# Attention and a squared-ReLU layer on one core: each store of two half blocks of tokens as two transfers of 64 rows

## The chip, the core and the metric

The kernel runs on one NeuronCore of a Trainium2 chip. The core has a matrix engine (TensorE, PE in the profile, its weight loads PEld), a vector engine (VectorE, DVE), a scalar engine (ScalarE, ACT), a general one (GpSimd, POOL), and a queue processor (SyncE, SP) that only issues transfers. Transfers run on 16 DMA engines that all queues share. The metric is device microseconds of one launch; lower is better.

## What is computed

Sliding-window attention with linear distance biases (8 sequences, 8 heads, 576 positions, head size 64, window 128), then a two-layer network on all 4608 tokens, with ReLU squared between the layers. Everything comes and goes in float32.

```python
scores = scale * np.matmul(q, k.transpose(0, 1, 3, 2))
mask = (rel >= 0) & (rel < window)
scores = np.where(mask, scores + bias[None], -1000000000.0)
attn = softmax(scores)                      # written out in the original
x = np.matmul(attn, v) ...reshape(B * S, H * D)      # 4608 x 512
h = x @ w_in                                # 512 x 2048
r = np.maximum(h, 0.0)
return (r * r) @ w_out                      # 2048 x 512
```

## The kernel before, in words

**Blocks and ranges.** Each sequence of 576 tokens is four blocks of 128 tokens and a half block of 64. The kernel pairs the half blocks of two sequences, so that they fill one range of 128 columns together: `ranges` holds 36 ranges of 128 tokens, 32 of them one block each and four of them two half blocks (ranges 14, 21, 28 and 32). Four ranges make a group of 512 tokens, and there are nine groups, 0 to 8. The half blocks thus stand in group 3 (third range), 5 (second), 7 (first) and 8 (first).

**Stages.** For each block PE multiplies q and k (line 643), ACT takes the exponential (L670), DVE multiplies by the mask of biases (L678), PE multiplies by v (L750), and DVE divides by the sums (L778) into a tile `x`. GpSimd loads k, q and v and casts them to bfloat16 on the way (L523, L528). From block 8 on, SP transposes k and q by DMA into `kqT` (L569, `DMA_TRANSPOSE`) and `x` into `xT` (L785). The first layer, "up", is lines 897, 915 and 996; from group 6 on it uses Strassen's seven products in Winograd's form, for which DVE makes differences of `xT` in tiles `ut` (L963). ACT and DVE make ReLU and square. The second layer, "down", is L1072 for group 0 and, from group 1 on, Strassen's seven products again (`product`, L1176), with sums of the activations made by DVE (L1297).

**Down and its stores.** Each product of a group adds into one of the output's quarters, 256 tokens by 256 columns. DVE or ACT copies or adds these into a tile `osb` of 128 partitions by 512 float32: its first 256 columns belong to one range of 128 tokens, its second 256 to the next. Each finished quarter is stored by `store` inside `product` (L1205 to L1214): products 2 and 3 finish the two column halves of a group's first two ranges, products 7 and 4 those of its last two. `places` says where the rows go. When both ranges are plain blocks at a fitting distance, one transfer covers (row, range, column), 256 KB. Otherwise each range has a transfer of its own, 128 KB in rows of 1 KB: a plain block is 128 rows of `out`, and a range of two half blocks is one transfer over (half, row, column), L1114 to L1116: the two halves stand d rows apart in `out`, and together they are the 128 partitions of the tile's half. There are eight such transfers, two for each of the four half-block ranges; in their pattern on the side of `out` the half, of size 2, is the outermost dimension.

Seven of the eight are issued by SP; the one of group 8's product 3 is issued by ACT (`end`). The last group's last product goes to `last_product`, which stores its two ranges, both plain blocks, in three pieces (L1274), two from SP and one from ACT. Stores of group 0 are at L1098.

**What sets the order.** The whole program is first a list of tasks, each with the engines that could run it, a cost in ns, a key, the tasks that it needs and the buffers that it takes and frees. `Plan.order` (L167 to L263) goes through them as a list scheduler: on each engine it takes, of the tasks that could start, the one with the smallest key. A table `ADJ` moves single keys. The result is a fixed order of instructions for each engine. For a transfer, the cost in `engs` is how long its queue is taken to be busy (530 for a store, 1200 to 1500 for a transpose), and `dma` is how long the transfer is taken to fill the DMA engines:

```python
            if t.dma is not None:
                at = max(st + self.FIRST[e], self.dma_free)
                self.dma_free = at + t.dma
                t.end = self.dma_free + (self.LAND[e] if t.lat is None else t.lat)
            ...
            free[e] = st + dur
```

A tile `osb` (a ring of five) is free again at the store's planned `end`; on the chip, when the store has landed. Each queue issues in its order: when an issue waits or takes long, what is behind it waits too. Transfers from SP and ACT take turns with eight semaphores, so each also waits until the transfer eight before it has landed.

Of the kernel before, what the change touches and what calls it, by code (L numbers as in the profile page):

```python
# [266 lines left out]
def kernel(  # L267
    ctx: ExitStack, tc: tile.TileContext, q, k, v, moe_w_in, moe_w_out, out
):
    nc = tc.nc  # L270
# [29 lines left out]
    at = {x: m for m, x in enumerate(seq)}  # L300
# [43 lines left out]
    plan = Plan({**psum_bufs, "rec": 4, "rt": RT, "g": 2, "osb": OSB, "cs": CS, "ut": 2, "s1": 1, "s2": 1, "v0": B, "kqT0": B, "stage": 2, **size})  # L344

    def bank(slot, name):
        slot.tile = psum.tile([128, 512], FP32, tag=slot.tag, bufs=psum_bufs[slot.tag], name=name)
        return slot.tile
# [18 lines left out]
    def dve_p(n, rate=1):  # L367
        return n / rate / 0.96 + 72.0

    def mm(n):  # L370
        return max(n, 66) / 2.4 + 2.5
# [36 lines left out]
    for part in (1, 0):  # L408
        key = EARLY + 2 if part else -1e5 + 1100
# [127 lines left out]
    for what, key in at_first.items():  # L537
        n = int(what[1:])
# [563 lines left out]
    def places(r, n):  # L1102

        rows = [[b * S + kb * 128 for b, kb in ranges[r + i]] for i in range(n)]
        if n == 2 and len(rows[0]) == len(rows[1]) == 1:
            lo, d = rows[0][0], rows[1][0] - rows[0][0]
            if d >= 128 and lo + 2 * d <= NT:
                return [((0, 1), lambda w: out[lo:lo + 2 * d, w].rearrange("(j p) c -> p j c", p=d)[0:128])]
        to = []
        for j, x in enumerate(rows):  # L1110
            if len(x) == 1:
                to.append(((j,), lambda w, x=x: out[x[0]:x[0] + 128, w]))
            else:
                d = x[1] - x[0]  # L1114
                lo = x[0] + 64 - d
                to.append(((j,), lambda w, lo=lo, d=d: out[lo:lo + 2 * d, w].rearrange("(h p) c -> h p c", p=d)[:, d - 64:d]))  # L1116
        return to

    t_ws = []
# [24 lines left out]
    def product(g, p, z, key):  # L1144
# [60 lines left out]
        def store(name, t, hi, tok, end=False):  # L1205
            so = st["slot"][name]
            w = slice(hi * 256, hi * 256 + 256)
            for i, (j, to) in enumerate(places(4 * g + tok, 2)):
                def run(j=j, to=to):
                    (nc.scalar if end else nc.sync).dma_start(  # L1210
                        to(w), so.tile.rearrange("p (j c) -> p j c", j=2)[:, j[0]] if len(j) == 1 else
                        so.tile.rearrange("p (j c) -> p j c", j=2))
                plan.add({"ACTQ" if end else "SP": 530.0}, key, run, [t], [], [so], dma=340.0 * len(j), lat=1000.0,
                         name=f"st{g}.{p}.{tok + i}")  # L1214

        def combine(name, what, deps, free, tok, hi, label, end=False):
            so = st["slot"][name]

            def run():
                what(so.tile)  # L1220
            t = plan.add({"DVE": dve_p(512)}, key, run, deps, [], free, name=f"{label}_{g}")
            store(name, t, hi, tok, end)
            return t

        if p == 1:
            snap("s1", [])
        elif p == 2:
            combine("s1", lambda o: nc.vector.tensor_tensor(o, slot.tile, o, op=ALU.add), both + [st["s1"]], [slot],
                    0, 0, "c11")
        elif p == 6:  # L1230
            snap("s2", [])
        elif p == 5:
            snap("s5", [])
        elif p == 7:
            if g == NG - 1:
                snap("s3", [slot])
            st["c22"] = combine("s5", lambda o: nc.vector.tensor_tensor(o, slot.tile, o, op=ALU.add),
                                both + [st["s5"]], [slot], 2, 1, "c22")
        elif p == 3:
            combine("s2", lambda o: nc.vector.tensor_tensor(o, slot.tile, o, op=ALU.add), both + [st["s2"]], [slot],  # L1240
                    0, 1, "c12", g == NG - 1)
        else:
            snap("s3", [slot])
            store("s3", st["s3"], 0, 2)

    def last_product(g, z, key, st, stationary):

        F = FCB // 2
        cuts = [(0, 256)] if z == 0 else [(0, LAST), (LAST, 256)]
        for lo, hi in cuts:  # L1250
            slot = Slot("a")

            def emit(slot=slot, lo=lo, hi=hi):
                bank(slot, "o")
                for c in range(F):
                    nc.tensor.matmul(slot.tile[:, 0:hi - lo], stationary(c), wsum[:, 3, c, lo:hi],
                                     start=c == 0, stop=c == F - 1)
            tm = plan.add({"PE": F * mm(hi - lo)}, key, emit,
                          g_sq_at(g)(1, (2, 3)) + [t_ws[0][3], t_ws[1][3], st["P", 3, 1], st.get("tail")],
                          [slot], [g_slots[g]], name=f"p{g}.4.{z}" + ("b" if lo else ""))  # L1260
            st["tail"] = tm
            so = st["slot"]["s3"]

            def run(slot=slot, lo=lo, hi=hi):
                o = so.tile[:, z * 256 + lo:z * 256 + hi]
                nc.vector.tensor_tensor(o, o, slot.tile[:, 0:hi - lo], op=ALU.add)
            t = plan.add({"DVE": dve_p(hi - lo)}, key, run, [tm, st["s3"]], [], [slot],
                         name=f"c21.{z}.{lo}_{g}")

            q = z == 1 and lo == 0  # L1270

            def store(lo=lo, hi=hi, q=q):
                to = places(4 * g + 2 + z, 1)[0][1]
                (nc.scalar if q else nc.sync).dma_start(to(slice(lo, hi)), so.tile[:, z * 256 + lo:z * 256 + hi])  # L1274
            plan.add({"ACTQ" if q else "SP": 530.0}, key, store, [t], [], [so], dma=340.0 * (hi - lo) / 256, lat=1000.0,
                     name=f"st{g}.4.{z}" + ("b" if lo else ""))

    def g_sq_at(g):
        def sq(half, parts):
            return [x for t in (2 * half, 2 * half + 1) for p in parts for x in sq_of[g, t, p]]  # L1280
        return sq
# [76 lines left out]
```

## Time and profile before

| | |
|---|---|
| three runs | 305.5, 305.91, 306.91 us (median 305.91) |
| the profiled execution, whole | 305.41 us |
| its span, first to last instruction | 303.5 us |
| PE busy | 288.1 us (95%) |
| DVE, ACT, POOL busy | 241.6, 205.7, 106.4 us |
| mean granted clock of PE | 0.997 |
| stores of lines 1205 to 1214 | 37 from SP, 2 from ACT |
| issue time of those from SP: least, median, most | 0.345, 0.532, 3.582 us |
| landing of those that the profile tells: least, median, most | 1.7, 2.1, 12.9 us |
| last PE instruction, last DVE instruction end | 296.9, 297.2 us |

Times within the execution are in us from the span's start. The profile has a page and further views of the same trace: who waited for whom, the chain of work that ended last, the instructions in order of time, and tables by stretches of time. In them a row names line, engine, operation, and the tiles written and read (out<-in); "SPq" and "ACTq" are queue instructions, which only issue a transfer. The difference between span and whole time, 1.9 us, lies around the program.

### The profile page before, as it was taken

The numbers are of one execution on the slowest core, as the hardware profiler recorded it, in microseconds if no ns is written. First come the engines' busy times: TensorE is split into PE (matmuls) and PEld (weight loads), VectorE is DVE, ScalarE is ACT, GpSimd is POOL, SyncE is SP. The second block draws the span as 40 slices with busy tenths as digits, with TensorE's granted clock in tenths as the row PEclk, the third lists the DMA queues.
The fourth block names the chain that finished last, engine by engine and source line by source line (L and its number), as shares of the span: only waits on it lengthen the run. The fifth ranks groups of instructions, "written<-read, shape, count | busy, mean of one in ns | idle before, by whom it ended". The sixth has DMA issues, their size and how long they took to land.

```text
span 303.5 us, 8328 instructions
## 1 busy us (share of the span) xinstructions
PE 288.1 (95%) x3311; PEld 224.8 (74%) x3311; DVE 241.6 (80%) x624; ACT 205.7 (68%) x394; POOL 106.4 (35%) x132
## 2 busy tenths in 40 slices
PE   6989999997999999999999999899999999999991
PEld 2679755986887887556657866468898888888880
DVE  4584666779985899798969993999999998899841
ACT  3685444577486674894988567696997689789510
POOL 8953398263462774525725502360000000000000
PEclk9999999999999999999999999999999999999998
DMA  9999999999999999999999999999203301110223
GB/s 132 145 202 206 184 187 165 150 156 154 160 160 183 160 162 157 189 153 133 164 155 164 178 145 74 192 151 184 86 14 103 48 35 41 67 35 2 85 71 90
DMA packets 170312, 39.62 MB, mean 131 GB/s; under 512 B 156320, under 2 KB 169760, under 8 KB 170272
## 3 DMA queue, kind: packets, MB, share of 16 engines
q0 software_dynamic: 115184, 18.10, 84.6%
q1 hardware_dynamic: 54382, 20.39, 44.2%
q10 hardware_dynamic: 706, 0.59, 0.7%
q8 instruction: 26, 0.43, 0.6%
q14 instruction: 14, 0.11, 0.2%
HBM read 36.70 MB, written 9.44 MB: 152 GB/s over the span
## 4 chain that ended last, share of the span: by engine, by line
PE 73%; DMA 16%; POOL 4%; DVE 3%; SPq 1%; issue 1%; ACT 0%; POOLq 0%; DVEq 0%
PE o L1176 31%; PE h L996 12%; PE h L915 12%; DMA w_out_sb<-in_moe_w_out_dram 6%; PE h L897 6%; DMA xT<-x 5%; PE pv L750 5%; PE s L643 5%; DMA vf<-in_v_dram 3%; DMA w_in_sb<-in_moe_w_in_dram 2%; POOL kq L523 2%; POOL vf L528 2%; DVE x L778 1%; PE o L1072 1%; SPq L785 1%
## 5 line engine op out<-in xcount | busy, mean ns | idle before, releaser
L858 ACT ACTIVATE rt<-h 128x512 bf16<-128x512 f32 (+1 forms) x109 | 64.3, 597 | 37.3 <-PE h L897 17.5
L670 ACT ACTIVATE P<-s 128x512 bf16<-128x512 f32 x120 | 64.2, 605 | 9.6 <-PE s L643 9.6
L1176 PEld LDWEIGHTS <-g 128*128 128x128 bf16 x624 | 59.8, 98 | 9.3
L523 POOL DMA_DIRECT2D kq<-in_k_dram x39 | 33.3, 854 | 73.4 <-DMA kqT<-kq 65.6
L870 DVE TENSOR_TENSOR g<-rt 128x512 bf16<-128x512 bf16 (+1 forms) x99 | 40.8, 418 | 18.8 <-ACT rt L858 16.8
L1176 PE MATMUL o<-w_out_sb,g 128*128 128x256 bf16 x384 | 47.5, 273 | 0.0
L897 PE MATMUL h<-xT,w_in_sb 128*128 128x128 bf16 (+1 forms) x512 | 46.6, 246 | 0.5 <-DMA xT<-x 0.5
L915 PE MATMUL h<-xT,w_in_sb 128*128 128x512 bf16 x192 | 46.0, 380 | 0.0
L897 PEld LDWEIGHTS <-w_in_sb 128*128 128x128 bf16 x512 | 38.6, 98 | 4.7 <-issue 0.7
L678 DVE TENSOR_TENSOR P<-P,masks 128x512 bf16<-128x512 bf16 x96 | 39.0, 421 | 3.1 <-ACT P L670 0.9
L523 POOL DMA_DIRECT2D kq<-in_q_dram x39 | 33.2, 851 | 7.5 <-PE h L897 3.8
L1176 PE MATMUL o<-wsum,sums 128*128 128x256 bf16 x256 | 31.6, 273 | 1.2 <-DVE sums L1297 1.2
L778 DVE TENSOR_TENSOR x<-pv,rec 128x256 bf16<-128x256 f32 (+1 forms) x80 | 31.3, 415 | 0.6
L528 POOL DMA_DIRECT2D vt<-in_v_dram x32 | 26.9, 850 | 13.6 <-PE pv L750 11.0
L1176 PE MATMUL o<-wsum,g 128*128 128x256 bf16 x240 | 30.7, 273 | 0.0
L915 PEld LDWEIGHTS <-w_in_sb 128*128 128x128 bf16 x192 | 17.3, 98 | 17.6
L868 ACT ACTIVATE g<-rt 128x512 bf16<-128x512 bf16 x46 | 29.0, 632 | 1.3
L1176 PEld LDWEIGHTS <-sums 128*128 128x128 bf16 x256 | 24.5, 98 | 4.8 <-DVE sums L1297 1.4
L750 PEld LDWEIGHTS <-P 128*128 128x128 bf16 (+1 forms) x576 | 22.8, 100 | 6.0 <-issue 2.1
L1017 DVE TENSOR_TENSOR vf<-h,vf 128x512 f32<-128x512 f32 x36 | 24.4, 688 | 2.9 <-PE h L996 1.1
L858 ACT ACTIVATE rt<-vf 128x512 bf16<-128x512 f32 x36 | 22.3, 625 | 3.6 <-DVE vf L1017 3.6
L377 ACT ACTIVATE osb<-o 128x512 f32<-128x512 f32 x19 | 11.4, 598 | 17.2 <-PE o L1176 17.2
(82 smaller groups left out, 392.6 us busy)
## 6 DMA issues: line engine op xcount, KB each, us to landing
out_dram<-osb SPq DMA_DIRECT2D x27, 256.0 KB, 3.1
kq<-in_k_dram POOLq DMA_DIRECT2D x31, 128.0 KB, 7.7
kq<-in_q_dram POOLq DMA_DIRECT2D x31, 128.0 KB, 8.8
vt<-in_v_dram POOLq DMA_DIRECT2D x24, 128.0 KB, 8.6
w_out_sb<-in_moe_w_out_dram POOLq DMA_DIRECT2D x4, 512.0 KB, 16.2
out_dram<-osb SPq DMA_DIRECT2D x15, 128.0 KB, 7.3
w_in_sb<-in_moe_w_in_dram POOLq DMA_DIRECT2D x3, 512.0 KB, 12.4
vf<-in_v_dram POOLq DMA_DIRECT2D x8, 128.0 KB, 6.0
```

The costliest lines, as they stand in the source:

```text
L523: nc.gpsimd.dma_start(view(kq[s_kq[m].idx], i), source(src, m, split))
L528: nc.gpsimd.dma_start(tile_of(s_v[m])[0:n, :, 0:D], source(v, m))
L670: nc.scalar.activation(flat(Pt[sP.idx]), sS[i].tile.rearrange("p (j t) -> p j t", j=2)[:, :, lo:hi], AF.Exp, bias=0.0, scale=scale)
L678: nc.vector.tensor_tensor(flat(Pt[sP.idx]), flat(Pt[sP.idx]), flat(masks), op=ALU.mult)
L750: nc.tensor.matmul(sv.tile[0:n, hi * (D + 1):(hi + 1) * (D + 1)], prob, tile_of(s_v[mk])[:, h, 0:D + 1], start=mk == parts[0][1], stop=mk ...
L778: nc.vector.tensor_tensor(o, heads(sv)[0:n, :, 0:D], sr.tile[0:n, :].unsqueeze(2).to_broadcast([n, 4, D]), op=ALU.mult)
L858: nc.scalar.activation(srt.tile[:, 0:n], i, AF.Relu, bias=0.0, scale=1.0)
L870: nc.vector.tensor_tensor(o, i, i, op=ALU.mult)
L897: nc.tensor.matmul(slot.tile[:, f * w:(f + 1) * w], w_in_sb[:, cc, fc * 128:(fc + 1) * 128], xT[:, cc, lo % (XR * 128):lo % (XR * 128) + w ...
L915: nc.tensor.matmul(slot.tile, w_in_sb[:, cc, fc * 128:(fc + 1) * 128], xT[:, cc, g * 512 % (XR * 128):g * 512 % (XR * 128) + 512], start=c ...
L996: nc.tensor.matmul(slot.tile[:, j * 256:j * 256 + 256], a, b_, start=fresh and j == 0 and c == 0, stop=c == 1, skip_group_check=True)
L1176: nc.tensor.matmul(slot.tile[:, z * 256:z * 256 + 256], stationary(c), moving(c), start=fresh and z == 0 and c == 0, stop=c == F - 1, skip ...
```

## The change

A range of two half blocks is stored as two transfers of 64 rows each, one for each half, in place of one transfer over (half, row, column). `places` now gives for each transfer of `store` a list of (first partition, partitions, rows of `out`): one entry for a plain block or a pair of blocks, two entries for two half blocks. `store` issues them one behind the other from the same queue, and the planner's cost of such a store on its queue becomes 530 for each entry (its `dma` cost stays). In `last_product` the loop has one entry, as both its ranges are plain.

```diff
             if d >= 128 and lo + 2 * d <= NT:
-                return [((0, 1), lambda w: out[lo:lo + 2 * d, w].rearrange("(j p) c -> p j c", p=d)[0:128])]
+                return [((0, 1), [(0, 128, lambda w: out[lo:lo + 2 * d, w].rearrange("(j p) c -> p j c", p=d)[0:128])])]
         to = []
         for j, x in enumerate(rows):
-            if len(x) == 1:
-                to.append(((j,), lambda w, x=x: out[x[0]:x[0] + 128, w]))
-            else:
-                d = x[1] - x[0]
-                lo = x[0] + 64 - d
-                to.append(((j,), lambda w, lo=lo, d=d: out[lo:lo + 2 * d, w].rearrange("(h p) c -> h p c", p=d)[:, d - 64:d]))
+            n = 128 // len(x)
+            to.append(((j,), [(n * i, n, lambda w, r=r, n=n: out[r:r + n, w]) for i, r in enumerate(x)]))
         return to
...
                 def run(j=j, to=to):
-                    (nc.scalar if end else nc.sync).dma_start(
-                        to(w), so.tile.rearrange("p (j c) -> p j c", j=2)[:, j[0]] if len(j) == 1 else
-                        so.tile.rearrange("p (j c) -> p j c", j=2))
-                plan.add({"ACTQ" if end else "SP": 530.0}, key, run, [t], [], [so], dma=340.0 * len(j), lat=1000.0,
+                    parts = so.tile.rearrange("p (j c) -> p j c", j=2)
+                    for p, n, at in to:
+                        (nc.scalar if end else nc.sync).dma_start(
+                            at(w), parts[p:p + n, j[0]] if len(j) == 1 else parts[p:p + n])
+                plan.add({"ACTQ" if end else "SP": 530.0 * len(to)}, key, run, [t], [], [so], dma=340.0 * len(j), lat=1000.0,
                          name=f"st{g}.{p}.{tok + i}")
...
             def store(lo=lo, hi=hi, q=q):
-                to = places(4 * g + 2 + z, 1)[0][1]
-                (nc.scalar if q else nc.sync).dma_start(to(slice(lo, hi)), so.tile[:, z * 256 + lo:z * 256 + hi])
+                for p, n, at in places(4 * g + 2 + z, 1)[0][1]:
+                    (nc.scalar if q else nc.sync).dma_start(at(slice(lo, hi)),
+                                                            so.tile[p:p + n, z * 256 + lo:z * 256 + hi])
```

## The prediction

> **What bounds the kernel now.** I began with the page's slices, to see which engine has no rest and where:
>
> ```profile
> PE   6989999997999999999999999899999999999991
> ...
> DMA  9999999999999999999999999999203301110223
> ```
>
> TensorE (PE) stands at 9 nearly everywhere, so from the fifth slice on only a hole in PE can be won. The end is different: in the last slice PE is at 1, while DMA still works. Next I asked who waited. The answers, for PE and for VectorE (DVE) from 100 us on and for SyncE's queue (SP) over the whole run, hold these rows:
>
> ```profile
> PE s L643 <- DVE x L778: 1.5, 1, 1.5
> ...
> DVE ut L963 <- DMA xT<-x: 4.9, 1, 4.9
> ...
> SPq L1353 <- DMA out_dram<-osb: 4.5, 1, 4.5
> ```
>
> PE has one hole after 100 us, of 1.5 us; DVE stood still for 4.9 us for a transpose of x; and at the end SP waits 4.5 us for stores. The chain of waits between 180.86 and 193.6 us ties the first two together:
>
> ```profile
> 180.86 8.78 DMA xT<-x
> ...
> 189.76 0.44 DVE ut L963
> ...
> 191.94 0.98 DVE x L778 x3
> 192.93 0.61 PE s L643 x16
> ```
>
> One transpose issued at 180.86 takes 8.78 us. DVE is stuck behind it, works off its queue, and PE gets its operands at 192.93 (the hole is 1.47 us, 191.44 to 192.91).
>
> **What the stores have to do with it.** The table by stretches says how many DMA engines work; its last two columns are the busy share of 16 engines and GB/s:
>
> ```profile
> 255.45:256.45 1.00, 1.00 (x12) 0.90 (x10) 0.69 (x2) 1.00 (x3) 0.00 (x0) 1.00 0.74 262
> 179.00:184.20 5.20, 5.20 (x55) 2.97 (x54) 4.62 (x14) 4.89 (x10) 0.74 (x1) 1.00 1.39 41
> 217.00:220.50 3.50, 3.50 (x61) 2.96 (x59) 3.37 (x9) 3.40 (x8) 0.00 (x0) 1.00 0.12 37
> ...
> 300.25:302.00 1.75, 0.00 (x0) 0.00 (x0) 0.00 (x0) 0.00 (x0) 0.00 (x0) 0.93 0.12 39
> ```
>
> At 255.45 a whole store of two blocks (256 KB, outermost dimension 128) moves in 1 us. At 217 us a store over (half, row, column) is alone on the queue (issued 216.04, 128 KB): 0.12 x 16 = 1.9 engines, 3.5 us, 37 GB/s. Two engines do 64 rows each, as many as its outermost dimension, the half. The other two rows run at the same rate: 179 to 184.2 us (issued 171.59; the share there is swollen by long records of other packets, the 41 GB/s are what counts), and the end of the program. A single block of 128 rows, issued 229.88, landed after 1.7 us. So eight stores, two halves times four half blocks, sit on two of sixteen engines.
>
> The Trainium skill, "DMA: Bandwidth & Descriptors", section "Why a DMA increments its semaphore by 16 and not by 1", says that the engines used are the largest number up to 16 that divides the slowest dimension of both sides; for (2, 64, c) that is 2, which the 1.9 engines agree with, and for 64 rows it would be 16.
>
> **The change part by part.** *Issues.* Eight issues become sixteen. In quiet stretches one over the halves takes 0.53 to 0.55 us on SP, a plain block alone 0.345, behind another 0.45 to 0.47. Two plain ones are 0.80 at the middle of these, so +0.25 us of SP each. On SP this lies beside PE work: SP is off PE's path except through its transposes. If the cover went, seven times 0.25 would be 1.8 us.
>
> *The stage at 168 us* (group 3: two half stores, two plain ones, one pair).
>
> ```profile
> 168.54 7.26 SPq L1210 DMA_DIRECT2D out_dram<-osb  x5
> 175.91 6.88 SPq L785 DMA_TRANSPOSE xT<-x  x3
> 182.96 5.72 SPq L569 DMA_TRANSPOSE kqT<-kq  x2
> ```
>
> Five stores take 7.26 us here because the plain block behind each half store takes 1.61 and 3.58 us to issue. The transposes follow at once, and between 179.0 and 184.2 us nothing but the two-engine store moves (41 GB/s, in a queue that before and after does 170 to 280). The new stores have the rows outermost, as the plain block that landed in 1.7 us has; from that row I take it that 64 rows spread too, 4 to an engine. So the queue should come free about 5 us earlier (184.2 less 179.0), and the transpose that landed at 189.64 also. PE could run at 191.44; it needs 1.5 us of these 5. I take the whole hole, **-1.47**. Bounds: 0, if the queue stays clogged by the loads (DMA is at 9 in these slices), and -1.47, since PE is busy for 102.88 of the 102.9 us from 194 us to its end and nothing more can be won. Late next would be PE's own product behind it, for which the operands are there. The half stores of groups 5 and 7 have no waiter: the transposes at 233 to 237 us are used at 260, and PE has no hole.
>
> *The end.* The last issues are these:
>
> ```profile
> 294.75 0.37 SPq L1210 DMA_DIRECT2D out_dram<-osb  x1
> ...
> 295.87 1.54 ACTq L1210 DMA_DIRECT2D out_dram<-osb  x2
> 296.02 0.74 DVE L1266 TENSOR_TENSOR osb<-osb,o 128x256 f32<-128x256 f32 x2 [0.18 <-PE o L1256]
> 296.51 1.07 SPq L1274 DMA_DIRECT2D out_dram<-osb  x2
> 296.92 0.29 DVE L1266 TENSOR_TENSOR osb<-osb,o 128x128 f32<-128x128 f32 x1 [0.16 <-PE o L1256]
> 297.51 0.41 ACTq L1274 DMA_DIRECT2D out_dram<-osb  x1
> ```
>
> The half store is ScalarE's (ACT) first at 295.87 (1.14 us to issue, then 0.36 for the plain one). By the landing events fourteen engines finish the very last store at 300.2 to 300.7, the other two at 301.8 and 302.2: on those it queues behind 64 rows. The issue at 297.23 needs 4.8 us to land where alone 1.7 (one block) to 2.1 (a pair) is usual. After the change ACT issues three. The first takes between 0.36 (a plain one) and 1.14 (today's); I take 0.95, since 0.19 of today's 1.14 is what the form costs more on SP (0.54 against 0.345) and the rest looks like ACT's first issue since the program's start. With 0.36 for each of the next two and today's gaps, the last issue goes out at 297.7 (between 297.1 and 297.9). With 1.9 us to land (1.7 to 2.7, the last being what today's fourteen engines need) it is done at 299.6 in place of 302.2: **-2.5** (bounds -1.6 to -3.1; in the warm case SP's issue at 297.23 is the last). What follows, 1.3 us to 303.5, stays.
>
> *The order.* The planner is told 530 ns more for each split SP store. Following its rules through its own list, I find that the entry behind is the pair's other part, or starts later than the longer issue ends, but for group 5's last store (+0.4 us); no transpose moves. Only the places of the last ACT and SP issues change. I cost this at 0; what hides it is that SP has gaps there. A moved order would cost up to the holes PE had when it waited for masks and sums at 73 to 76 us (0.8 + 1.2).
>
> *Sum.* 1.47 + 2.5 = 4.0. The profiled execution took 305.41 (span 303.5), so 301.4. The three runs have a median of 305.91, 0.5 higher; I add half of that and forecast **301.7 us**.
>
> **Rivals.**
> *The end alone:* the hole at 192 stays, because the loads keep the DMA engines full. For it: DMA at 9 until 205 us. Against: 41 GB/s where that store is alone. 305.4 - 2.5 + 0.25 = 303.2.
> *The hole alone:* three issues on ACT and a late landing eat the end (last issue 297.9, landing 2.7 and a second of contention). 304.2.
> *It does not spread:* 64 rows could be put on few engines; no run here has a plain store of 64 rows. Then only issues are added, +0.36 on ACT: 306.1, the same.
> *Halves serialize:* the Trainium skill, same page, section "Rules for kernel authors", advises against two transfers to disjoint halves, since both spread over the same sixteen engines, and for one of 128 rows. As a mechanism of this kernel it would add an issue and gain no landing, 305.4 + 0.36 + 0.25 = 306.0, if today's store used sixteen engines; the 1.9 engines speak against it.
> *Slower:* the long issues at 169 and 172 us belong to the full queue and not to the half store ahead, so that each added issue takes as long. Two more of 3.58 us put the transpose of 189.64 at 196.8, and PE's hole grows by 7.2: 305.4 + 7.2 - 2.5 = 310.1. It decides from a delay of 2.5 us on. Against: another plain store of a pair in a full queue, at 207.29, took 1.38, and issues behind no half store at 112 to 115 us, also in full slices, 0.54 to 0.61.
>
> **How the numbers follow.** Forecast 0.65, the end alone 0.16, the hole alone 0.07, no spread or serialized halves 0.07, slower 0.05. The range takes the forecast's bounds (305.4 - 1.47 - 3.1 = 300.8) and the first rival with its own (305.9 - 1.6 = 304.3, of which I leave the last third out): 300.7 to 304.0. What can be told from no change here is 0.5%, 1.5 us, so faster means below 304.4: forecast, the end alone, most of the hole alone, 0.87; same 0.08; slower 0.05.
>
> **What would show it.** Right: no stretch left in which only about two engines move (179 to 184, 217 to 220.5, 300 to 302 above); no DVE wait of 4.9 us at L963 and no PE hole at L643; SP's last wait for stores near 2 us and not 4.5. Wrong: the issues of the seven stores at 168 us together longer than 7.26 us; landings of the last stores still over 4 us; or new PE holes between 100 and 290 us, which would mean that the order changed.

## The result, and the profile after

The kernel after takes 301.65 us (median of four runs, 301.38 to 302.25), the kernel before 306.3 us beside it (305.5 to 306.91): a ratio of 0.9853, 95% interval 0.9822 to 0.9883, so 4.5 us less (3.6 to 5.5). The two profiled executions are 305.41 and 301.38 us, their spans 303.5 and 299.5. No computation changed, and the order of instructions on every engine is that of before, apart from the added issues; the lines after `places` have moved up by a few (L1176 is now L1172, L1210 is L1208, L1274 is L1271).

The slices of the page after, to be held against those of before:

```profile
PE   6989999997999999999999999999999999999994
```

The reader is to see two digits in PE's row: the 8 in the 26th slice, where the hole was, is a 9, and the last slice has a 4 in place of a 1, since the span ends sooner after PE's end. Asked who waited from 100 us on, the profile has no row for PE any more, and none for DVE at L963. What is left of SP's wait for the last stores is

```profile
SPq L1351 <- DMA out_dram<-osb: 1.8, 1, 1.8
```

which was 4.5. The stretches show what became of the two-engine transfers (stretch and length; per engine busy time and count; granted clock, busy share of the 16 DMA engines, GB/s):

```profile
179.00:184.20 5.20, 5.20 (x55) 2.95 (x54) 4.62 (x15) 4.89 (x11) 0.50 (x1) 1.00 1.72 142
...
296.00:298.00 2.00, 0.00 (x0) 0.00 (x0) 0.00 (x0) 0.00 (x0) 0.00 (x0) 1.00 0.76 242
```

142 GB/s stand where there were 41, and in the last two microseconds of the stores 242 GB/s at a share of 0.76, where the end of before had 39 at 0.12. The issues of the stage at 168 us in order of time:

```profile
169.05 4.20 SPq L1208 DMA_DIRECT2D out_dram<-osb  x7
174.64 4.65 SPq L785 DMA_TRANSPOSE xT<-x  x3
```

Seven stores take 4.20 us where five took 7.26, and the transposes behind them are issued in 1.2 to 1.4 us each; the last of the three for `xT` lands at 183.68, against 189.64. Of these 6.0 us, 2.8 are its earlier issue (178.07 against 180.86) and 3.2 its shorter way from issue to landing (5.61 against 8.78). DVE is not held up, and PE runs through. The end:

```profile
294.58 1.86 ACTq L1208 DMA_DIRECT2D out_dram<-osb  x3
...
296.55 0.38 ACTq L1271 DMA_DIRECT2D out_dram<-osb  x1
```

ACT now issues three transfers in 1.86 us, so its last issue goes out 0.97 us after PE's end (295.58) and not 0.63 us after it; it lands in 1.6 us.

The 4.03 us between the two profiled executions divide at PE's end: it comes 1.30 us earlier (296.88 to 295.58: the same matmuls start 0.24 us later than before from 102 us on, ahead of every changed store, and 1.30 us earlier from 195.5 us on, so 1.54 us go with the hole), and from PE's end to SP's last wake-up it is 2.63 us and not 5.36, so 2.73 us less.

### The profile page after: what moved, and what is told of

Its sections match the earlier page's. It is cut to its first block, busy times and chain, and to the rows that moved or that the text cites. A ratio compares the mean times of both kernels' runs of the same rounds, so it can differ in the third digit from the quotient of the medians.

```text
span 299.5 us, 8343 instructions
## 1 busy us (share of the span) xinstructions
PE 288.5 (96%) x3311; PEld 224.6 (75%) x3311; DVE 241.9 (81%) x624; ACT 205.8 (69%) x394; POOL 106.5 (36%) x132
## 4 chain that ended last, share of the span: by engine, by line
PE 80%; DMA 11%; POOL 4%; DVE 2%; issue 1%; ACT 1%; POOLq 0%
PE o L1172 32%; PE h L915 14%; PE h L996 12%; PE h L897 9%; DMA w_out_sb<-in_moe_w_out_dram 6%; PE pv L750 6%; PE s L643 5%; DMA vf<-in_v_dram 3%; DMA w_in_sb<-in_moe_w_in_dram 2%; POOL kq L523 2%; POOL vf L528 2%; PE o L1072 1%; PE o L1253 1%; DVE x L778 0%; DVE g L870 0%
## 5 line engine op out<-in xcount | busy, mean ns | idle before, releaser
L1172 PEld LDWEIGHTS <-g 128*128 128x128 bf16 x624 | 59.8, 98 | 9.3
L1172 PE MATMUL o<-w_out_sb,g 128*128 128x256 bf16 x384 | 47.5, 273 | 0.0
L1172 PE MATMUL o<-wsum,sums 128*128 128x256 bf16 x256 | 31.6, 273 | 1.2 <-DVE sums L1295 1.2
L1172 PE MATMUL o<-wsum,g 128*128 128x256 bf16 x240 | 30.7, 273 | 0.0
L1172 PEld LDWEIGHTS <-sums 128*128 128x128 bf16 x256 | 24.5, 98 | 4.8 <-DVE sums L1295 1.4
```

The source lines that it names most:

```text
L1172: nc.tensor.matmul(slot.tile[:, z * 256:z * 256 + 256], stationary(c), moving(c), start=fresh and z == 0 and c == 0, stop=c == F - 1, skip ...
```

## The experiments

Times of before scatter by about a per cent from run to run, so each ratio stands with its interval, and the trace is read for what it shows exactly: the hole and the wait at the end. Part of the scatter lies ahead of every changed store: in the fourteen traces PE is idle for about 4.5 to 7.2 us in the first 100 us. Each ratio is against runs of before taken beside the experiment; their medians are 305.28 us (for the end, group 3, the other five and the cut by columns), 305.75 (62 rows, quarters, ACT's queue, SP's share) and 305.84 (the control and the three runs with it). The quotient of the medians differs from the ratio by up to 0.3%. "Last wait" is SP's for the stores; "tail" is the time from PE's end to its last wake-up.

**Which of the eight stores matter.** Three kernels split some of them only:

```diff
-    def places(r, n):
+    def places(r, n, split=False):
...
-            n = 128 // len(x)
-            to.append(((j,), [(n * i, n, lambda w, r=r, n=n: out[r:r + n, w]) for i, r in enumerate(x)]))
+            if len(x) == 1 or split:
+                n = 128 // len(x)
+                to.append(((j,), [(n * i, n, lambda w, r=r, n=n: out[r:r + n, w]) for i, r in enumerate(x)]))
+            else:
+                d = x[1] - x[0]
+                lo = x[0] + 64 - d
+                to.append(((j,), [(0, 128, lambda w, lo=lo, d=d: out[lo:lo + 2 * d, w].rearrange("(h p) c -> h p c", p=d)[:, d - 64:d])]))
...
-            for i, (j, to) in enumerate(places(4 * g + tok, 2)):
+            for i, (j, to) in enumerate(places(4 * g + tok, 2, (g, p) == (8, 3))):
```

This is the end alone; for the stage at 168 us the condition is `g == 3`, for the other five stores `g in (5, 7) or (g, p) == (8, 2)`. The diffs of the experiments are against the kernel after, but for one, which says so.

*The end alone.* Expected:

> Only group 8's product 3, the store that ACT issues at the end, is split in two halves of 64 rows; the other seven keep the form of before. Theory (two places, independent): SP's last wait falls from 4.5 to about 1.9 us, the hole of 1.5 us at PE's scores stays, 306.3 - 2.7 = 303.6 us. Rival (the gain at the end is one gain with the middle, for instance a matter of all eight): 301.7 or 306.3 us.

Measured: 303.76 us, ratio 0.9919 (0.988 to 0.9959), 2.5 us less by the ratio and 1.5 by the medians. PE waited (from 100 us on: line, what ended the wait, us in total, times, longest)

```profile
PE s L643 <- DMA kqT<-kq: 2.1, 1, 2.1
```

and SP for the stores

```profile
SPq L1356 <- DMA out_dram<-osb: 1.9, 2, 1.7
```

The hole is there, the last wait is short. The end is a gain of its own.

*The stage at 168 us alone.* Expected:

> Only the two stores of group 3's half-block range (the stage at 168 us) are split; the other six keep the form of before. Theory: the wait of DVE for the transpose of x (4.9 us at L963) and the hole of 1.5 us in PE go, the last wait of SP stays at 4.5 to 4.6 us; 306.3 - 1.4 = 304.9 us. Rival (the hole comes from the loads that fill the DMA engines, and went for another reason): hole stays, 306.3 us.

Measured: 304.37 us, ratio 0.9974 (0.9942 to 1.0006). In the trace DVE has no wait at L963 and PE no hole after 100 us, and the last wait is that of before:

```profile
SPq L1356 <- DMA out_dram<-osb: 4.4, 2, 4.2
```

The mechanism came out, the size of it not clearly: 0.8 us, and the interval holds both nothing and 1.4. It was run again (below).

*The other five.* Expected:

> Only the stores of groups 5 and 7 and the one of group 8's product 2 are split, five of the eight. Theory: nobody waits for them, so 306.3 us, within 0.3; hole and last wait as before. Rival (five stores that land earlier free tiles and the queue for something): 0.5 us or more below that.

Measured: 304.76 us, ratio 0.9965 (0.9936 to 0.9993), 1.1 us less by the ratio and 0.5 by the medians, where nothing was expected. The trace gave no reason in the changed stores: hole of 0.96 us, DVE's wait of 4.1 us at L963, last wait 4.3. So this too was run again.

**The same once more, with a control.** The kernel before against itself:

> The kernel before, unchanged, against itself: ratio 1.000. How far the ratio and the interval stray from that says how much a difference of 0.3% to 0.4% in the other runs is worth.

The kernel after:

> The kernel after, unchanged, on this chip: ratio 0.9853 as before (0.982 to 0.988), 4.0 to 4.5 us less than the kernel before; no hole of PE after 100 us, last wait 2.6 us after PE's end.

The other five, and group 3:

> The same kernel as the one in which only the five stores of groups 5, 7 and 8 (product 2) are split, which came out at 0.9965 (0.9936 to 0.9993) where 1.000 was expected. Theory (nobody waits for these five): ratio 1.000, within 0.003, and in the trace hole and last wait as before. Rival (they bring something, for instance because the last store's queue is empty earlier): 0.9965 again, and a last wait that is shorter than that of the kernel before in the same call by 0.5 us or more.

> The same kernel as the one in which only the two stores of group 3 are split, which came out at 0.9974 (0.9942 to 1.0006) where 0.9953 (1.4 us) was expected. Theory (the hole of 1.47 us goes, all of it is won): 0.995, 1.4 us. Rival (the hole goes, but half of it comes back as other idle time of PE): 0.9975, and in the trace more idle time of PE elsewhere.

Measured, in this order: 0.9994 (0.9958 to 1.003), 0.9873 (0.9829 to 0.9917), 0.9988 (0.9955 to 1.0021), 0.9944 (0.9915 to 0.9973). In the traces, the kernel after again has no hole, and a tail of 2.59 us; that of the other five has a hole of 1.02 us and a tail of 5.37 us, against 5.49 in the control; that of group 3 has no hole. So the other five bring nothing that can be told from the control (0.24% as a mean of two runs, so a small gain is not excluded), and group 3 alone is worth 0.41% as a mean of its two runs, 1.25 us. The parts add up: 0.81% at the end and 0.41% at 168 us are 1.2%, against 1.5 and 1.3% for the whole change.

The control taught more than its ratio. Its profiled execution, of the very kernel before, shows no wait of DVE at L963 and no hole at 192 us; its only row for PE after 100 us is

```profile
PE h L915 <- DMA xT<-x: 0.7, 1, 0.7
```

and that wait is at 119.5 us, long before this stage. Yet the two-engine stretch is there, and at its usual rate (stretches and issues of the control):

```profile
177.00:181.00 4.00, 3.95 (x65) 2.51 (x66) 4.00 (x10) 2.92 (x6) 0.00 (x0) 1.00 0.78 35
```

```profile
166.44 6.28 SPq L1210 DMA_DIRECT2D out_dram<-osb  x5
174.54 5.24 SPq L785 DMA_TRANSPOSE xT<-x  x3
```

The stores went out 2.1 us earlier than in the first profile (166.44 against 168.54), the slow stretch ended at 181.2 and not 184.2, and the transposes landed at 185.25 against 189.64; DVE went on to them at 185.37 without a wait. The slow stretch is in both traces (4.0 and 5.2 us); whether PE loses by it is another matter. Going out early is not enough. In the first run of the other five, which has the hole, the second slow store was issued at 171.09 us, before the control's (171.65), and the transposes from 174.50 on, as in the control (174.54); yet the last one landed at 188.78.

The landing events show what else differs: GpSimd's loads of k and q. In the six traces with the hole, GpSimd issued the last load of this stage at 173.2 to 175.6 us, and it landed at 187.7 to 190.8; in the control it was issued at 169.7 and landed at 183.4. Such a load has sixteen landing events, which I read as one for each engine, and two of them come late (before, issued 173.48: fourteen by 179.8, two at 189.8). So these loads are late on two engines as well. That the loss hangs on how much is queued there beside the slow store fits all these traces, but no run varied it by itself. Of the seven traces of kernels that store group 3's half blocks over two engines from SP, six have the hole (0.96 to 2.07 us) and this one has none; of the six traces that spread them, none has it.

**Is it the engines, or the number and size of transfers?** Sixteen transfers as after, but cut by columns:

```diff
...
-            n = 128 // len(x)
-            to.append(((j,), [(n * i, n, lambda w, r=r, n=n: out[r:r + n, w]) for i, r in enumerate(x)]))
+            if len(x) == 1:
+                to.append(((j,), [(slice(0, 256), lambda w, x=x: out[x[0]:x[0] + 128, w])]))
+            else:
+                d = x[1] - x[0]
+                lo = x[0] + 64 - d
+                to.append(((j,), [(slice(z, z + 128), lambda w, lo=lo, d=d, z=z: out[
+                    lo:lo + 2 * d, w.start + z:w.start + z + 128].rearrange("(h p) c -> h p c", p=d)[:, d - 64:d])
+                    for z in (0, 128)]))
...
-                    for p, n, at in to:
+                    for cols, at in to:
                         (nc.scalar if end else nc.sync).dma_start(
-                            at(w), parts[p:p + n, j[0]] if len(j) == 1 else parts[p:p + n])
+                            at(w), parts[:, j[0], cols] if len(j) == 1 else parts)
...
```

> The eight stores of half-block ranges become sixteen as in the change, but each covers (half, row, 128 columns), so its outermost dimension is still the half. Theory (the number of DMA engines that carry the store is what counts): still two engines, now with 128 packets of 512 B each instead of 64 of 1 KB, so the hole of PE at 192 us and the wait of SP for the last stores (4.5 us before) both stay or grow; 306 to 308 us, against 306.3 before and 301.65 after. Rival (smaller transfers, or twice as many of them, is what helps): about 301.7 us, last wait near 2 us.

Measured: 306.08 us, ratio 1.0022 (0.9986 to 1.0057). DVE waited

```profile
DVE ut L963 <- DMA xT<-x: 5.5, 1, 5.5
```

and SP, for the last stores,

```profile
SPq L1356 <- DMA out_dram<-osb: 5.0, 1, 5.0
```

both longer than before, and the seven stores at 168 us took 13.1 us to issue. As many transfers as in the change, of the same 64 KB, and nothing is won.

**Is it the pattern over halves?** Plain rows, but a number of them that no larger count of engines divides:

```diff
-            n = 128 // len(x)
-            to.append(((j,), [(n * i, n, lambda w, r=r, n=n: out[r:r + n, w]) for i, r in enumerate(x)]))
+            cut = [(0, 128)] if len(x) == 1 else [(0, 62), (62, 2)]
+            to.append(((j,), [(64 * i + k, n, lambda w, r=r + k, n=n: out[r:r + n, w]) for i, r in enumerate(x)
+                              for k, n in cut]))
...
```

> Each half is stored as a transfer of 62 rows and one of 2 rows (plain patterns, rows outermost, no dimension of halves; the planner's cost kept as in the change). The Trainium skill, DMA: Bandwidth & Descriptors, section Why a DMA increments its semaphore by 16 and not by 1, has the engines used as the largest number up to 16 that divides the slowest dimension: two for 62 rows. By that the store is on two engines again, 31 rows of each half on each, as slow as before, though no pattern over halves is left: 306 to 308 us. Rival (the pattern over halves is what is slow, rows always spread): two more issues a half store than after, as with quarters, 302.9 us.

Measured: 305.04 us, ratio 0.9998 (0.9968 to 1.0027): the change's whole gain is gone, with 62 of 64 rows of each half stored by a plain pattern. Each of the 62-row stores has only two late landing events, the last of them 2.8 and 4.5 us after the issue for the two at the end; DVE waited 4.3 us at L963, PE has a hole of 1.2, SP's last wait is 4.1. The forecast of 306 to 308 was set against 306.3 for before; beside this run before took 305.75, and the result is level with that. In the stretch from 180 to 184 us:

```profile
180.00:184.00 4.00, 4.00 (x41) 2.37 (x36) 3.31 (x11) 3.76 (x8) 1.16 (x2) 1.00 0.39 45
```

So it is neither the halves nor the count of transfers, but on how many engines the rows fall.

**Do more issues cost?** Four transfers of 32 rows for each half-block range:

```diff
+            x = x if len(x) == 1 else [r + 32 * i for r in x for i in range(2)]
             n = 128 // len(x)
...
```

> Each store of a half-block range as four transfers of 32 rows (the planner's cost kept as in the change, so the order stays). Theory: 32 rows still go over sixteen engines, so no hole comes back; what is added is issues, two more of some 0.6 us ahead of the last ACT issue (1.2 us at the end), and on SP at 168 us four more, 2.4 us, which the transposes have to spare (they landed 6 us earlier after the change than before): 301.65 + 1.2 = 302.9 us. Rival (splitting itself is what helps, the finer the better): 301.7 us or less. Other rival (issues on SP decide): a hole in PE near 190 us, 304 us or more.

Measured: 301.69 us, ratio 0.988 (0.9844 to 0.9916), the same as after within the intervals. No hole; eleven stores at 168 us took

```profile
167.90 8.16 SPq L1209 DMA_DIRECT2D out_dram<-osb  x11
176.16 4.67 SPq L785 DMA_TRANSPOSE xT<-x  x3
```

8.16 us, more than the 7.26 of before, and the three transposes landed at 180.9 to 183.1 all the same. This clears the SP queue's issues: what hurt at 168 us was not that SP was busy for 7 us but that the engines were not. At the end ACT's five stores took 2.25 us against 1.86 for three, and the tail is 3.00 us against 2.63. Of the 1.2 us that I expected to lose there, this trace shows 0.37: an issue of 32 rows took 0.36 to 0.44 us, one of 64 rows 0.56 to 0.61.

**Is it SP's queue, or the engines?** The kernel before, with the two slow stores of group 3 issued by ACT (a diff against before):

```diff
-                def run(j=j, to=to):
-                    (nc.scalar if end else nc.sync).dma_start(
+                aq = end or (g == 3 and tok + i == 2)
+
+                def run(j=j, to=to, aq=aq):
+                    (nc.scalar if aq else nc.sync).dma_start(
...
-                plan.add({"ACTQ" if end else "SP": 530.0}, key, run, [t], [], [so], dma=340.0 * len(j), lat=1000.0,
+                plan.add({"ACTQ" if aq else "SP": 530.0}, key, run, [t], [], [so], dma=340.0 * len(j), lat=1000.0,
```

> The kernel before, with the two two-engine stores of group 3 issued by ACT instead of SP; nothing is split. Theory A (what blocks is SP's queue: its transposes stand behind the two-engine store in the same queue): DVE's wait of 4.9 us and PE's hole of 1.5 us go, 306.3 - 1.4 = 304.9 us, last wait still 4.5 us. Theory B (the two engines themselves are the bottleneck, whoever issues): the transposes still need these two engines, land as late as before, hole stays, 306.3 us.

Measured: 304.6 us, ratio 0.9978 (0.9942 to 1.0014). DVE's wait and the hole at 192 us are absent, which reads like theory A. It is not shown, though. The three transposes for `xT` still landed only behind the slow store (its last event at 182.50, theirs at 182.90, 183.37 and 184.88); DVE had other work until 186.2, and GpSimd's last load was out early (issued 169.35, landed 182.73), as in the control, which had no hole either. And while the second slow store moved, the other queues stood nearly still (the view of DMA between 178 and 181 us; q10 is ACT's queue, q1 SP's, q0 GpSimd's):

```profile
DMA packets 247, 0.12 MB, mean 40 GB/s; under 512 B 158, under 2 KB 247, under 8 KB 247
...
q1 hardware_dynamic: 77, 0.02, 49.9%
q10 hardware_dynamic: 89, 0.09, 10.5%
q0 software_dynamic: 81, 0.01, 5.2%
```

SP's transposes, issued at 178.09 and 179.38, got 77 packets through in 3 us (some of them recorded as very long, hence the share), where SP's queue moves some 500 to 600 a microsecond right after. So a two-engine store in ACT's queue holds up SP's as well. By what is not settled: the two engines that each transpose also needs, or something else that both queues share. GpSimd's load issued at 169.35 was late on two engines only (fourteen landing events by 175.4, the others at 180.8 and 182.7), but of each transpose all sixteen events come together, within 0.2 us. So no part of a transpose was finished early on the other fourteen engines, which the two engines alone do not explain.

**Is there more at the end?** The kernel after, with one half from SP:

```diff
-                        (nc.scalar if end else nc.sync).dma_start(
+                        (nc.scalar if end and p == 0 else nc.sync).dma_start(
```

> The kernel after, with the second half of group 8's product 3 issued by SP, which has nothing to issue between 293.8 and 295.2 us, instead of ACT. Theory (at the end the landing follows ACT's row of four issues of 0.4 to 0.6 us): ACT's last issue moves 0.6 us forward, SP's last store becomes the last to land, 0.65 us less: 301.0 us. Rival (the transfers themselves fill the engines at the end): 301.65 us, the same.

Measured: 301.29 us, ratio 0.989 (0.9828 to 0.9952) against before, no different from after. ACT's last issue is earlier, 0.50 us after PE's end in place of 0.97, but the stores land in 1.9 to 2.6 us in place of 1.6 to 2.1, and the tail is 2.65 us. The last store is issued 0.47 us earlier and takes 0.49 longer to land. That fits the rival, by which the end is bound by moving the six transfers and not by the row of issues; what made the landing longer the trace does not show.

## Why the prediction was right, point by point

The forecast was 301.7 us, the measured median is 301.65, and the span forecast for the profiled execution (301.4 less the 1.9 around it) is the measured 299.5. That they agree to 0.05 us is luck: the difference is known to about 1 us either way, and the half of 0.5 us that the forecast added was a guess. Two deviations inside it nearly cancel, so the points matter more than the sum.

*Two of sixteen engines.* Right, and shown three ways: each 64-row store has sixteen separate landing events where the old ones had one early (about 1 us after the issue) and two late ones; columns cut over the same two engines gain nothing; 62 rows, plain, fall back. The Trainium skill's rule ("DMA: Bandwidth & Descriptors", section "Why a DMA increments its semaphore by 16 and not by 1") is borne out for an outermost dimension of 2, 32, 62 and 64.

*The hole, -1.47.* In the profiled pair it went as forecast, by the chain named: the transposes landed 6.0 us earlier (5 were expected). What the step lacked is that it was read from one execution. The control has the slow stretch and no hole, so the step is worth 1.47 in that execution, and that is no fixed sum: the holes of the seven traces go from 0 to 2.07 us, and the two runs of group 3 alone give 1.25 us, each known to about 0.9 us on either side, which does not set it apart from 1.47. Two readings in this step do not hold. The 170 to 280 GB/s around the slow stretch are those ahead of it; behind it, from 184.2 to 186 us, 81 GB/s moved. And the transposes at 233 to 237 us are used not first at 260, by PE, but at 243.06, by DVE (L963); the last of them had landed at 240.97, so they still had no waiter.

*The end, -2.5.* Measured -2.73 in the profiled pair, and 2.5 (1.3 to 3.7) in time for the end alone (1.5 by its medians). Its terms were off both ways. The first ACT issue takes 0.56 us and not the 0.95 I took: I had put most of its 1.14 down to ACT's first store as such, but it belongs to the old form (below). The next two take 0.61 each and not 0.36, since they follow at once. The last issue is thus 0.97 us after PE's end, where I had 0.8, and it lands in 1.62 and not 1.9.

*Issues.* I gave +0.25 us of SP for each split store. At 288 to 290 us the two halves take 0.47 and 0.60, and the plain block behind them 0.58, together 1.65 us against 1.01 for the pair before, so +0.64. It was hidden as I said, and on SP more than that was with the quarters.

*The order.* As worked out: the same on every engine.

*The rivals.* The end alone and the hole alone were each made and are each a part. "Does not spread" (by its own terms 306.0 and not 306.1) and "halves serialize" are refuted by the landing events. The latter is the advice of the Trainium skill, same page, section "Rules for kernel authors", not to split a transfer into disjoint halves. It presumes that the undivided transfer spreads over all engines, which the one here did not; the quarters, which lose 0.37 us at the end and nothing measurable in time against the halves, show that on spread transfers such a split is at least cheap here. "Slower" supposed that the long issues at 169 and 172 us came from a full queue; after the change seven stores take 0.41 to 0.59 us each in the same full slices. A long issue needs no slow store, though: in the second run of group 3 alone the first of the seven took 1.74. The slow store ahead does not lengthen the issue every time either: in the control the same two plain blocks took 0.42 and 0.46.

## What to carry to other kernels

Look for stretches in which the DMA engines have work queued and move little (35 to 48 GB/s here, where spread stores did 142 to 262), and then at the outermost dimension of what is moving: a store that looks like one tidy transfer ran here on two engines, as many as that dimension has entries. What it cost here was not its own landing, but what stood behind it, in other queues too: transposes, and through them DVE's order and PE; and at the end of the program, everything. And a hole seen in one execution is worth its length times how often it happens: profile the unchanged kernel a second time before pricing it.

## What the runs showed of the hardware that was not expected

- A store on two engines holds up transfers in other queues: with it in ACT's queue, SP's transposes passed 77 packets in 3 us, and loads that GpSimd issued at about the same time as such a store on SP's queue landed 10 us later on two engines than on the other fourteen (before, issued 173.48).
- ACT's first store over (half, row, column) takes 1.14 to 1.15 us to issue (eight traces), its second 0.57 (two traces), its third 0.52 (one trace). As a first store of 64 plain rows ACT takes 0.55 to 0.56 us. So on ACT the 0.6 us more come with the first use of that form, and not with the engine's first store.
- A store of 64 rows that is issued right behind another mostly takes 0.58 to 0.61 us in quiet stretches (the second half of group 7's product 3 took 0.70 to 0.95 in five traces), one of 32 rows mostly 0.41 to 0.44; alone, 0.47 to 0.50 and 0.31 to 0.36. Landing is mostly 1.9 to 2.1 us for 64 rows, and 1.5 to 1.6 for 32.
